# Layer 1's weight transfers on GpSimd's queue, one weight chunk made per block, and most convolution taps in the block-end step

## The chip, the cores and the metric

The kernel runs on one core of a Trainium2 chip. The metric is the time of one execution on the device in microseconds, as the median of several runs. Engines are named as in the profile: PE is TensorE, DVE is VectorE, ACT is ScalarE, POOL is GpSimd, and SP is the engine whose queue issues nearly all DMA transfers. SPq is that queue.

## The reference

A causal convolution with seven softmaxed taps per head runs over 8192 tokens of 192 features. Two layers follow, each with 2048 hidden units: the first with SiLU, the second with ELU.

```python
def reference(**kwargs):
    attn_out = _attn_ref(**attn_kwargs)        # softmax(weight) taps over 7 tokens, per head
    x = attn_out.reshape(B * S, D)             # 8192 x 192
    x = _moe_ref(x=x, **moe_kwargs)            # h = x @ w_in; (h * sigmoid(h)) @ w_out
    return _moe2_ref(x=x, **moe2_kwargs)       # h = x @ w_in; (h if h > 0 else exp(h) - 1) @ w_out
...
```

The kernel splits each float32 operand into a high and a low part and adds up three products (high by high, and the two mixed ones).

## The kernel before

**Tiling.** The tokens are cut into 16 blocks of 512 (`TB`), the hidden units into 8 chunks of 256 (`NQ`). A unit is (layer, block, chunk), and there are 256 of them. A *step* is what the main loop emits for one unit: the products h of this unit with the first weights (`in_products`, 18 of L547), the activation and the split of its result (`act_steps`), and the products of an earlier unit with the second weights. The units run in this order: blocks 0 and 1 of layer 0 together, chunk by chunk (steps 0 to 15); then blocks 2 to 15 of layer 0, 8 steps each (steps 16 to 127); then layer 1's 16 blocks (steps 128 to 255). In a block, q counts the chunks.

**Two forms.** Up to block 2 the low part of the hidden values is kept in float32 form (`g_lo`, L576, products at L720 and L628). From block 3 on it is scaled to a half-precision number (`lo`, L584) and multiplied later: `high_products` (L647) run three steps after the unit's h, and once a block, in the step with q = 2 of the next block, the low parts of all eight chunks follow (`low_products`, L659 for c and L671 for ab). This is the *block-end step*. In it, ScalarE and VectorE also add up the two row halves of the sums (`end_steps`, L771 and L762; `emit_end_c`, L796 and L798) and store them (L376, L380). The hidden values h have two buffers in PSUM. A buffer is free when VectorE's `lo` has read it, so the products of step s wait for `lo` of step s - 2.

**Scales.** The scale of a block's hidden values comes from a bound. `measure` (L428) takes the maxima of a block on each partition, `share` (L418) stores them, `fetch` (L422) brings all of them to every partition, and `set_scale` (L451 to L459) computes from them. The weights' maxima go the same way (`set_weight_scale`, `finish_weight_scale`). Layer 0's second weights are scaled afterwards, one chunk per step, in `rescale` (L245 to L251) and `rescale_end` (L257).

**Side work.** A table `fill` holds, for each step, small pieces of work that are emitted there, ahead of the step's activation, in the order in which `at` was called. These are, for each block b with first step s of layer 0: its input's load at s - 14; the 14 taps of its convolution (`conv_steps`: 7 of 512 columns, 7 of 256, L500 and L502), `measure` and the split into high and low parts (`split_conv`, L156 and L159), spread evenly over the seven steps from s - 10; `fetch` at s - 3; `set_scale` at s - 1. The crossings of x_hl (L315) copy one half of the partitions to the other, by SP.

**Layer 1's weights** arrive as float64 (I64 words) and are decoded on the chip. From step 40 on, each chunk is loaded and its maximum found (`load_w`, `measure_raw`, every third step). From step 72 on, every fifth step, a chunk is loaded again, decoded and split (`made_steps`, nine pieces in five steps), in a single pair of tiles (wi, wo). It is stored to DRAM (L203) and, when layer 0 is done with its own chunk, brought back in its place (`bring`, L221). The copy into wi (L364) of one chunk has to wait until the store of the chunk before has read the tile.

**Order.** The order is written out by hand, and each engine runs its instructions in program order, SP's queue too. For blocks 0 and 1, the two row halves use one bank in turn, and SP does a `nop` as a marker between them (L729), which TensorE waits for. `pair_end` (L743 to L749) ends these two blocks; its tile `other` has one buffer.

Of the kernel before, what the change touches and what calls it, by code (L numbers as in the profile page):

```python
# [9 lines left out]
F32 = mybir.dt.float32  # L10
# [35 lines left out]
def kernel(  # L46
# [48 lines left out]
    def w_loads(layer, q):  # L95
        w = weights[layer]

        def rows_of(i):
            if i == 0:
                raw_t[layer, q] = raw.tile([P, W_IN + W_OUT], I64, tag="raw", name="raw")  # L100
            nc.sync.dma_start(
                out=raw_t[layer, q][ROWS[i], 0 : 2 * P].rearrange("p (k m) -> p k m", k=2),
                in_=w[:, q, ts(i, P)].rearrange("(k p) m -> p k m", k=2),
            )

        def rest(cols):
            nc.sync.dma_start(out=raw_t[layer, q][:, cols], in_=w[:, q, cols])
# [73 lines left out]
    def made_steps(q):  # L181
# [15 lines left out]
        def send():  # L197
            if q == 0:
                wt[1, 0] = [wi, wo]
                return  # L200
            for n, t in (("wi", wi), ("wo", wo)):
                kept[n, q] = tc.dram_tile([P, 2, t.shape[2]], F32, name=f"kept_{n}")
                nc.sync.dma_start(out=kept[n, q], in_=t.bitcast(F32))  # L203

# [12 lines left out]
    def bring(q, k):  # L217
        name, n = (("wi", W_IN), ("wo", W_OUT))[k]
        t = wts.tile([P, 2, n], F32R, tag=f"{name}{q - 1}", name=name)
        wt.setdefault((1, q), [None, None])[k] = t  # L220
        nc.sync.dma_start(out=t.bitcast(F32), in_=kept[name, q])  # L221

# [32 lines left out]

# [158 lines left out]

    def share(key, t):

        shared[key] = tc.dram_tile([1, 2 * P], F32, name="shared")
        nc.sync.dma_start(out=shared[key].rearrange("a (p n) -> (a p) n", n=2), in_=t)  # L418

    def fetch(key):  # L420
        t = fixed.tile([P, 2 * P], F32, tag="all", name="all")
        nc.sync.dma_start(out=t, in_=shared[key].to_broadcast([P, 2 * P]))  # L422
        shared[key] = t
# [37 lines left out]
    def set_weight_scale(layer, of):  # L461
# [3 lines left out]
        if layer == 1:  # L465
# [3 lines left out]
            )  # L469
        share(layer, m)  # L470

# [228 lines left out]
    def pair_products(b, q):  # L700
# [37 lines left out]
        return [[lambda r=r, n=n: product(r, n) for n in range(len(order))] for r in range(2)]  # L738

    def pair_end(b):  # L740

        at, away = ROWS[:: 1 - 2 * b]
        c, ab = (acc_t.pop((0, b, name)) for name in ("c", "ab"))  # L743
        other = out_p.tile([P, TB], F32, tag="other", name="other")[at, :]
        copy(other, c[away, :])
# [68 lines left out]

    def at(step, f):
        fill.setdefault(max(step, 0), []).append(f)

# [23 lines left out]
    for b in range(2, NB):  # L841
        s = where[0, b, 0]
        if b > 2:
            at(s - 14, lambda b=b: pending.extend(x_loads(b)) if b < 5 else load_x(b))
        steps = [f for fs in zip(*(conv_steps(b, g) for g in range(2))) for f in fs]
        if b >= NEW:
            steps += [lambda b=b: measure(0, b, conv_t[b, 0], conv_t[b, 1])]
            at(s - 3, lambda b=b: fetch((0, b)))
            at(s - 1, lambda b=b: set_scale(0, b))
        steps += [lambda b=b, g=g: split_conv(b, g) for g in range(2)]  # L850
        spread(steps, *((s - 10, 7) if b > 2 else (s - 10, 8)))
# [17 lines left out]
    look += 3 * NQ  # L869
    at(look, lambda: set_weight_scale(1, found))  # L870
    at(look + 2, lambda: fetch(1))
    at(look + 4, lambda: finish_weight_scale(1))
# [12 lines left out]
    with tc.manual_schedule():  # L885
# [179 lines left out]
        for s in range(4, TWO + 3):  # L1065
# [24 lines left out]
        act = act_steps(units[TWO + 3])  # L1090
        run(fill.get(TWO + 3, ()))
        run(act)
# [3 lines left out]
        for s in range(TWO + 4, n_units):  # L1096
# [7 lines left out]
            act = act_steps(u)  # L1104
            if s == turn:
                run(fill.get(s, ()))
                run(act)
                continue
            done = units[s - (LATE if turn < s < n_units - 3 else LAG)]
            new = scaled(*done[:2])  # L1110
            if done[2] < NQ - 1:
                run(fill.get(s, ()))
                run(act)
                products(high_products(done) if new else out_products(done))
                continue
            if new:
                run(act)
                products(high_products(done))
# [6 lines left out]
            if not new:  # L1125
                run(act[1:])
            if u[0] == 0:
                end_ab()
                run(fill.get(s, ()))
            else:  # L1130
                run(fill.get(s, ()))
                end_ab()
            emit_end_c(*done[:2], both)

        products(high_products(units[-2]))
# [54 lines left out]
```

## Time and profile before

| | us |
|---|---|
| median of 3 runs | 1121.72 (1120.26 to 1122.46) |
| the profiled execution | 1120.85 |
| its span, first to last instruction | 1118.8 |
| PE busy | 1084.3 (97%) |
| DVE busy | 823.4 (74%) |
| ACT busy | 809.8 (72%) |
| POOL busy | 34.4 (3%) |
| mean granted PE clock | 0.991 of 2.4 GHz |

A busy PE is one with a matmul in flight. PE is busy in nearly every slice, so the 3% in which it is not, and the slower stretches behind them, are where time can be found without less work. Of DMA transfers, all go over one hardware queue, 81.17 MB, which takes 28.8% of the time of the 16 DMA engines. POOL works in the first 75 us only and issues no transfers.

### The profile page before, as it was taken

The numbers are of one execution on the slowest core, as the hardware profiler recorded it, in microseconds if no ns is written. First come the engines' busy times: TensorE is split into PE (matmuls) and PEld (weight loads), VectorE is DVE, ScalarE is ACT, GpSimd is POOL, SyncE is SP. The second block draws the span as 40 slices with busy tenths as digits, with TensorE's granted clock in tenths as the row PEclk, the third lists the DMA queues.
The fourth block names the chain that finished last, engine by engine and source line by source line (L and its number), as shares of the span: only waits on it lengthen the run. The fifth ranks groups of instructions, "written<-read, shape, count | busy, mean of one in ns | idle before, by whom it ended". The sixth has DMA issues, their size and how long they took to land.

```text
span 1118.8 us, 25134 instructions
## 1 busy us (share of the span) xinstructions
PE 1084.3 (97%) x10755; PEld 838.9 (75%) x10755; DVE 823.4 (74%) x1141; ACT 809.8 (72%) x899; POOL 34.4 (3%) x43
## 2 busy tenths in 40 slices
PE   9998899999998988999999999999999999999998
PEld 6887888676775666767877777787777778777776
DVE  8897867676685676776547777777777777777776
ACT  7765656555565575766668888888888898888885
POOL 4420000000000000000000000000000000000000
PEclk9999999999999898999999999999999999999999
DMA  5413113632435137331363212122221212222100
GB/s 156 129 44 76 35 34 91 130 89 80 117 95 149 56 90 172 70 105 39 81 202 97 58 36 54 27 57 58 58 57 35 47 36 57 57 59 57 35 13 23
DMA packets 54048, 82.77 MB, mean 74 GB/s; under 512 B 10800, under 2 KB 27312, under 8 KB 53936
## 3 DMA queue, kind: packets, MB, share of 16 engines
q1 hardware_dynamic: 53936, 81.17, 28.8%
q8 instruction: 84, 1.38, 0.6%
q14 instruction: 28, 0.23, 0.1%
HBM read 43.23 MB, written 18.12 MB: 55 GB/s over the span
## 4 chain that ended last, share of the span: by engine, by line
PE 76%; DVE 10%; DMA 6%; ACT 3%; issue 2%; SPq 2%; DVEq 0%; ACTq 0%
PE h L547 37%; PE ab L647 14%; PE ab L671 9%; PE c L647 7%; PE c L659 5%; DVE lo L584 3%; DVE conv L502 2%; DMA all<-shared 2%; DMA kept_wi<-wi 2%; PE ab L720 2%; PE c L720 1%; DMA x_hl<-x_hl 1%; DMA shared<-sum 1%; PE ab L628 1%; ACT g_hi L581 1%
## 5 line engine op out<-in xcount | busy, mean ns | idle before, releaser
L547 PE MATMUL h<-x_hl,wi 64*128 64x512 f32 x4464 | 583.2, 393 | 26.5 <-DVE lo L584 25.4
L547 PEld LDWEIGHTS h<-x_hl,wi 64*128 64x128 f32 x4464 | 440.7, 186 | 129.4 <-DVE lo L584 34.9
L593 DVE SCALAR_TENSOR_TENSOR g<-g,h 128x1024 f32<-128x1024 f32 x128 | 156.3, 1221 | 129.8 <-ACT g L592 129.8
L647 PE MATMUL ab<-g_hi,wo 64*128 64x512 f32 x1856 | 249.5, 388 | 0.0
L647 PEld LDWEIGHTS ab<-g_hi,wo 64*128 64x128 f32 x1856 | 176.0, 185 | 36.1
L584 DVE SCALAR_TENSOR_TENSOR lo<-h,forth,g_hi 128x1024 f16<-128x1024 f32 x104 | 133.2, 1281 | 76.7 <-ACT g_hi L581 76.3
L589 ACT ACTIVATE h<-h 128x1024 f32<-128x1024 f32 x104 | 104.8, 1007 | 100.3 <-PE h L547 99.1
L584 DVE SCALAR_TENSOR_TENSOR lo<-g,forth,g_hi 128x1024 f16<-128x1024 f32 x128 | 163.6, 1278 | 0.1
L591 ACT ACTIVATE g<-h 128x1024 f32<-128x1024 f32 x128 | 131.7, 1029 | 42.9 <-PE h L547 42.9
L647 PE MATMUL c<-g_hi,wo 64*128 64x512 f32 x928 | 144.2, 389 | 0.0
L581 ACT ACTIVATE g_hi<-g,forth 128x1024 fp32r<-128x1024 f32 x126 | 143.1, 1136 | 0.0
L592 ACT ACTIVATE g<-g 128x1024 f32<-128x1024 f32 x128 | 135.7, 1060 | 4.0
L581 ACT ACTIVATE g_hi<-h,forth 128x1024 fp32r<-128x1024 f32 x104 | 116.1, 1116 | 3.4
L502 DVE SCALAR_TENSOR_TENSOR conv<-x_raw,tap_w,conv 128x512 f32<-128x512 f32 (+1 forms) x174 | 103.1, 632 | 0.2
L647 PEld LDWEIGHTS c<-g_hi,wo 64*128 64x128 f32 x928 | 88.1, 186 | 18.5 <-issue 0.4
L671 PE MATMUL ab<-lo,w 64*64 64x512 f16 x1792 | 101.5, 376 | 0.0
L671 PEld LDWEIGHTS <-w 64*64 64x64 f16 x1920 | 56.0, 107 | 44.3
L659 PE MATMUL c<-lo,w 64*64 64x512 f16 x928 | 55.9, 379 | 0.0
L659 PEld LDWEIGHTS <-w 64*64 64x64 f16 x928 | 24.6, 107 | 27.6 <-issue 10.6
L574 ACT ACTIVATE g_hi<-h 128x1024 fp32r<-128x1024 f32 x22 | 22.5, 1024 | 27.9 <-PE h L547 27.9
L720 PE MATMUL ab<-g_hi,wo 64*128 64x512 f32 x128 | 35.4, 395 | 0.0
L771 ACT ACTIVATE o<-ab,back 128x512 f32<-128x512 f32 x16 | 11.0, 688 | 32.1 <-PE ab L671 27.0
(121 smaller groups left out, 764.6 us busy)
## 6 DMA issues: line engine op xcount, KB each, us to landing
x_hl<-x_hl SPq DMA_DIRECT2D x60, 256.0 KB, 3.8
raw<-in_w_dram SPq DMA_DIRECT2D x21, 512.0 KB, 5.5
raw<-in_w_dram SPq DMA_DIRECT2D x51, 128.0 KB, 4.0
x_raw<-in_xT_dram SPq DMA_DIRECT2D x16, 259.0 KB, 3.9
kept_ab<-mid_ab SPq DMA_DIRECT2D x16, 256.0 KB, 2.1
mid_ab<-kept_ab SPq DMA_DIRECT2D x16, 256.0 KB, 5.2
mid_c<-kept_c SPq DMA_DIRECT2D x32, 128.0 KB, 4.8
all<-shared SPq DMA_DIRECT2D x31, 128.0 KB, 4.3
```

The source lines that it names most:

```text
L502: nc.vector.scalar_tensor_tensor(out=y, in0=x, scalar=w, in1=y, op0=ALU.mult, op1=ALU.add)
L547: nc.tensor.matmul(out=h[:, r, :], lhsT=w[ROWS[r], w_lo, ts(of, P)], rhs=x_part(layer, b, 3 * x_lo + part)[ROWS[r], :], start=n == 0, stop ...
L581: nc.scalar.activation(out=hi, in_=g, func=ACTF.Copy, scale=s)
L584: nc.vector.scalar_tensor_tensor(out=lo, in0=g, scalar=s, in1=hi.bitcast(F32), op0=ALU.mult, op1=ALU.subtract)
L589: return [lambda: nc.scalar.activation(out=g, in_=h, func=ACTF.Silu), high, low]
L591: lambda: nc.scalar.activation(out=g, in_=h, func=ACTF.Relu, scale=-1.0),
L592: lambda: nc.scalar.activation(out=g, in_=g, func=ACTF.Exp, scale=-1.0),
L593: lambda: nc.vector.scalar_tensor_tensor(out=g, in0=g, scalar=-1.0, in1=h, op0=ALU.add, op1=ALU.max),
L647: nc.tensor.matmul(out=acc_t[layer, b, f"{name}{r}"], lhsT=wo[ROWS[r], i, ts(k, P)], rhs=hi[ROWS[r], i, :], start=q == 0 and n in (0, 2), ...
L659: nc.tensor.matmul(out=acc_t[layer, b, f"c{r}"][ROWS[i], :], lhsT=w16_t[layer, q][ROWS[r], i, P:D], rhs=g_t[u][1][ROWS[r], i, :], start=Fa ...
L671: nc.tensor.matmul(out=bank[ROWS[j], :], lhsT=w16_t[layer, q][ROWS[r], i, ts(j, HP)], rhs=g_t[u][1][ROWS[r], i, tokens], start=first and i ...
L720: ins = nc.tensor.matmul(out=acc_t[0, b, name][0 : cols.stop - cols.start, :], lhsT=wo[ROWS[r], i, cols], rhs=g_t[0, b, q][part][ROWS[r], ...
```

## The change

Layer 1's loads of weights, its stores of made chunks and the transfers that bring them back are issued by GpSimd. So are `share` and `fetch` of the two weight scales. The fill table gets three parts per step. In a block-end step, part 0 runs ahead of the activation (blocks of layer 0 in the old form: after it), part 1 between the end of c and the end of ab, and part 2 at the end of the step; in other steps the three run one after the other where the table ran before.

From block 5 on, two taps of the convolution run at q = 0 and q = 1 of the block before, and the other 12 in its block-end step: three in part 0, five in part 1, four in part 2. `measure` follows at q = 3, the split at q = 4. Block 4 keeps its even spread of taps over seven steps, with `measure`, split and `fetch` one step later. Layer 1's chunks are measured at eight chosen steps from 37 to 49, and one chunk is made per block from block 8 on (steps 61 to 122).

In `rescale`, the scaling of the low part goes to ScalarE and the addition to GpSimd; before, VectorE did both in one operation for each of two ranges. In `pair_end` both blocks use one tile.

```diff
     def w_loads(layer, q):
         w = weights[layer]
+        queue = nc.gpsimd if layer else nc.sync
...
-            nc.sync.dma_start(
+            queue.dma_start(
...
-                nc.sync.dma_start(out=kept[n, q], in_=t.bitcast(F32))
+                nc.gpsimd.dma_start(out=kept[n, q], in_=t.bitcast(F32))
...
-        nc.sync.dma_start(out=t.bitcast(F32), in_=kept[name, q])
+        nc.gpsimd.dma_start(out=t.bitcast(F32), in_=kept[name, q])
...
+        nc.scalar.activation(out=wo[:, :, D : 2 * D], in_=wo[:, :, D : 2 * D].bitcast(F32), func=ACTF.Copy, scale=up[0])
         for src, to in LOWS:
-            nc.vector.scalar_tensor_tensor(
-                out=wo[:, :, to], in0=wo[:, :, to].bitcast(F32), scalar=up[0], in1=more[:, :, src],
-                op0=ALU.mult, op1=ALU.add,
-            )
+            nc.gpsimd.tensor_add(out=wo[:, :, to], in0=wo[:, :, to].bitcast(F32), in1=more[:, :, src])
...
-        share(layer, m)
+        share(layer, m, nc.gpsimd)
...
+        if b == 0:
+            others.append(out_p.tile([P, TB], F32, tag="other", name="other"))
+        other = others[0][at, :]
...
-    def at(step, f):
-        fill.setdefault(max(step, 0), []).append(f)
+    def at(step, f, part=0):
+        fill.setdefault((max(step, 0), part), []).append(f)
...
+        if b <= 3:
+            spread(steps + found_it * (b == NEW) + splits, s - 10, 7 if b > 2 else 8)
+        elif b == 4:
+            spread(steps, s - 10, 7)
+            at(s - 4, found_it[0])
+        else:
+            for k, f in enumerate(steps):
+                step = s - 8 if k < 1 else s - 7 if k < 2 else s - 6
+                at(step, f, 0 if k < 5 else 1 if k < 10 else 2)
+            at(s - 5, found_it[0])
+        if b >= 4:
+            for f in splits:
+                at(s - 4 + (b == 4), f)
         if b >= NEW:
-            at(s - 3, lambda b=b: fetch((0, b)))
+            at(s - 3 + (b == 4), lambda b=b: fetch((0, b)))
             at(s - 1, lambda b=b: set_scale(0, b))
...
-        at(where[1, b, 0] - 6, lambda b=b: split_mid(b))
+        at(where[1, b, 0] - 6, lambda b=b: split_mid(b), 1)
...
-    at(TWO + 1, lambda: fetch(0))
+    at(TWO + 1, lambda: fetch(0, nc.gpsimd))
...
-    look = where[0, 5, 0]
-    for q in range(NQ):
-        at(look + 3 * q, lambda q=q: load_w(1, q))
-        at(look + 3 * q + 3, lambda q=q: measure_raw(q))
+    looks = [where[0, b, q] for b, q in ((4, 5), (4, 6), (5, 0), (5, 1), (5, 5), (5, 6), (6, 0), (6, 1))]
+    for q, s in enumerate(looks):
+        at(s - 4, lambda q=q: load_w(1, q), 2)
+        at(s, lambda q=q: measure_raw(q))
...
-        s = look + 8 + 5 * k
-        at(s - 7, lambda q=q: load_w(1, q))
-        at(s, lambda q=q: made.update({q: made_steps(q)}))
-        for i in range(9):
-            at(s + i // 2, lambda q=q, i=i: made[q][i]())
+        s = where[0, 8 + k, 0]
+        at(s - 10, lambda q=q: load_w(1, q), 2)
+        at(s - 4, lambda q=q: made.update({q: made_steps(q)}))
+        for i, step in enumerate((-3, -2, -1, 0, -1, -1, 1, 1, 2)):
+            at(s + step, lambda q=q, i=i: made[q][i](), 2 * (step == 2))
...
             if new:
+                run_fill(s, 0)
                 run(act)
                 products(high_products(done))
                 low_products(*done[:2])
...
             end_c()
             if not new:
                 run(act[1:])
-            if u[0] == 0:
-                end_ab()
-                run(fill.get(s, ()))
-            else:
-                run(fill.get(s, ()))
-                end_ab()
+                run_fill(s, 0)
+            run_fill(s, 1)
+            end_ab()
             emit_end_c(*done[:2], both)
+            run_fill(s, 2)
```

## Rows read from the trace of the kernel before

**Rows 1.** The chain that ended last: start us, us, what.
```profile
165.94 3.45 PE ab L671 x64
...
338.05 3.51 PE ab L671 x64
...
527.29 3.45 PE ab L671 x64
...
560.01 3.51 PE ab L671 x64
...
593.55 3.45 PE ab L671 x64
...
1084.45 3.45 PE ab L671 x64
```

**Rows 2.** Waits: who waited for whom, us in total, times, longest us.
```profile
PE h L547 <- DVE lo L584: 25.4, 18, 5.6
...
ACT wi L364 <- DMA kept_wi<-wi: 18.6, 4, 7.6
...
DVE total L451 <- DMA all<-shared: 7.3, 4, 2.1
```

**Rows 3.** Timeline, 340 to 366: start, us, engine, line, instruction, [idle before <- releaser].
```profile
364.70 1.65 PE L547 MATMUL h<-x_hl,wi 64*128 64x512 f32 x6 [5.63 <-DVE lo L584]
```

**Rows 4.** Stretch 364 to 369: PE, PEld, DVE, ACT, POOL busy, granted clock, DMA.
```profile
364.00:369.00 5.00, 4.30 (x20) 3.47 (x22) 4.83 (x12) 2.46 (x4) 0.00 (x0) 0.50 0.10 42
```

**Rows 5.** Timeline of PE and of SP's queue, steps 16 to 18.
```profile
77.96 0.39 PE L547 MATMUL h<-x_hl,wi 64*128 64x512 f32 x1
...
82.26 0.39 PE L547 MATMUL h<-x_hl,wi 64*128 64x512 f32 x1
...
86.21 0.34 SPq L418 DMA_DIRECT2D shared<-own  x1
...
86.66 0.49 PE L720 MATMUL c<-g_hi,wo 64*128 64x512 f32 x1 [2.18 <-SPq L729]
...
90.43 0.60 PE L547 MATMUL h<-x_hl,wi 64*128 64x512 f32 x1
```

**Rows 6.** Timeline of ACT and PE where `pair_end` runs.
```profile
96.58 0.59 ACT L364 ACTIVATE other<-c 64x512 f32<-64x512 f32 x1 [3.77 <-DMA kept_c<-other]
...
97.94 0.73 PE L628 MATMUL c<-g_hi,wo 64*128 64x512 f32 x3 [0.76 <-DVE other L746]
```

**Rows 7.** Timeline of DVE and PE at steps 26 to 28.
```profile
136.38 0.75 DVE L251 SCALAR_TENSOR_TENSOR wo<-wo,up,more 128x128 fp32r<-128x128 f32 x2
...
138.38 3.91 PE L547 MATMUL h<-x_hl,wi 64*128 64x512 f32 x18 [3.98 <-DVE lo L584]
```

**Rows 8.** Timeline of DVE and POOL, 24 to 56.
```profile
42.70 2.11 DVE L502 SCALAR_TENSOR_TENSOR conv<-x_raw,tap_w,conv 128x512 f32<-128x512 f32 x2
...
43.61 1.79 POOL L174 TENSOR_TENSOR wo<-val,wo 128x128 fp32r<-128x128 f32 x2
...
48.69 1.14 DVE L502 SCALAR_TENSOR_TENSOR conv<-x_raw,tap_w,conv 128x512 f32<-128x512 f32 x2
```

**Rows 9.** Timeline around the block-end step of block 14 of layer 0.
```profile
526.31 1.28 DVE L584 SCALAR_TENSOR_TENSOR lo<-h,forth,g_hi 128x1024 f16<-128x1024 f32 x1 [2.11 <-ACT g_hi L581]
...
531.50 0.75 DVE L762 SCALAR_TENSOR_TENSOR mid_ab<-ab,back,mid_ab 128x512 f32<-128x512 f32 x1 [2.70 <-ACT mid_ab L771]
532.17 1.80 DVE L502 SCALAR_TENSOR_TENSOR conv<-x_raw,tap_w,conv 128x512 f32<-128x512 f32 x3
...
534.20 2.20 PE L547 MATMUL h<-x_hl,wi 64*128 64x512 f32 x18
...
535.81 1.27 DVE L584 SCALAR_TENSOR_TENSOR lo<-h,forth,g_hi 128x1024 f16<-128x1024 f32 x1
...
537.60 2.20 PE L547 MATMUL h<-x_hl,wi 64*128 64x512 f32 x18
```

**Rows 10.** Groups by line: xcount | busy us, mean ns of one | idle before.
```profile
L148 DVE SCALAR_TENSOR_TENSOR val<-mag,val 128x768 int32<-128x768 int32 x12 | 11.5, 958 | 1.3
```

More of the change, by code (lines that the diff above doesn't have):

```diff
@@ L106, in rest @@
         def rest(cols):
-            nc.sync.dma_start(out=raw_t[layer, q][:, cols], in_=w[:, q, cols])
+            queue.dma_start(out=raw_t[layer, q][:, cols], in_=w[:, q, cols])
         parts = (slice(2 * P, W_IN), OUT) if layer == 0 and q < RAW else (slice(2 * P, W_IN + W_OUT),)
@@ L413, with share, fetch @@
     shared = {}
-    def share(key, t):
+    def share(key, t, queue=nc.sync):
         shared[key] = tc.dram_tile([1, 2 * P], F32, name="shared")
-        nc.sync.dma_start(out=shared[key].rearrange("a (p n) -> (a p) n", n=2), in_=t)
-    def fetch(key):
+        queue.dma_start(out=shared[key].rearrange("a (p n) -> (a p) n", n=2), in_=t)
+    def fetch(key, queue=nc.sync):
         t = fixed.tile([P, 2 * P], F32, tag="all", name="all")
-        nc.sync.dma_start(out=t, in_=shared[key].to_broadcast([P, 2 * P]))
+        queue.dma_start(out=t, in_=shared[key].to_broadcast([P, 2 * P]))
         shared[key] = t
@@ L738, in pair_products @@
         return [[lambda r=r, n=n: product(r, n) for n in range(len(order))] for r in range(2)]
+    others = []
     def pair_end(b):
@@ L743, in pair_end @@
         c, ab = (acc_t.pop((0, b, name)) for name in ("c", "ab"))
-        other = out_p.tile([P, TB], F32, tag="other", name="other")[at, :]
+        if b == 0:
+            others.append(out_p.tile([P, TB], F32, tag="other", name="other"))
+        other = others[0][at, :]
         copy(other, c[away, :])
@@ L813, with run_fill @@
     fill = {}
-    def at(step, f):
-        fill.setdefault(max(step, 0), []).append(f)
+    def at(step, f, part=0):
+        fill.setdefault((max(step, 0), part), []).append(f)
+    def run_fill(s, *parts):
+        for part in parts or range(3):
+            run(fill.get((s, part), ()))
     def spread(steps, first, n):
@@ L845 @@
         steps = [f for fs in zip(*(conv_steps(b, g) for g in range(2))) for f in fs]
+        found_it = [lambda b=b: measure(0, b, conv_t[b, 0], conv_t[b, 1])]
+        splits = [lambda b=b, g=g: split_conv(b, g) for g in range(2)]
+        if b <= 3:
[11 more added lines that the diff above has]
+                at(s - 4 + (b == 4), f)
         if b >= NEW:
-            steps += [lambda b=b: measure(0, b, conv_t[b, 0], conv_t[b, 1])]
-            at(s - 3, lambda b=b: fetch((0, b)))
+            at(s - 3 + (b == 4), lambda b=b: fetch((0, b)))
             at(s - 1, lambda b=b: set_scale(0, b))
-        steps += [lambda b=b, g=g: split_conv(b, g) for g in range(2)]
-        spread(steps, *((s - 10, 7) if b > 2 else (s - 10, 8)))
     for b in range(NB):
         at(where[1, b, 0] - 9, lambda b=b: load_mid(b))
-        at(where[1, b, 0] - 6, lambda b=b: split_mid(b))
+        at(where[1, b, 0] - 6, lambda b=b: split_mid(b), 1)
         at(where[1, b, 0] - 4, lambda b=b: fetch((1, b)))
@@ L864 @@
         at(TWO + LAG + 2 + q, lambda q=q: rescale_end(q))
-    look = where[0, 5, 0]
-    for q in range(NQ):
-        at(look + 3 * q, lambda q=q: load_w(1, q))
-        at(look + 3 * q + 3, lambda q=q: measure_raw(q))
[L869 to L872, printed above, removed]
+    looks = [where[0, b, q] for b, q in ((4, 5), (4, 6), (5, 0), (5, 1), (5, 5), (5, 6), (6, 0), (6, 1))]
+    for q, s in enumerate(looks):
+        at(s - 4, lambda q=q: load_w(1, q), 2)
+        at(s, lambda q=q: measure_raw(q))
+    look = looks[-1]
+    at(look + 1, lambda: set_weight_scale(1, found))
+    at(look + 3, lambda: fetch(1, nc.gpsimd))
+    at(look + 5, lambda: finish_weight_scale(1))
     made = {}
     for k, q in enumerate([*range(1, NQ), 0]):
-        s = look + 8 + 5 * k
-        at(s - 7, lambda q=q: load_w(1, q))
-        at(s, lambda q=q: made.update({q: made_steps(q)}))
-        for i in range(9):
-            at(s + i // 2, lambda q=q, i=i: made[q][i]())
+        s = where[0, 8 + k, 0]
[3 more added lines that the diff above has]
+            at(s + step, lambda q=q, i=i: made[q][i](), 2 * (step == 2))
     base = where[0, NB - 1, 0]
@@ L1082 @@
                 pending.extend(w_loads(0, s + 1))
-            run(fill.get(s, ()))
+            run_fill(s)
             run(act[-1:] if s < 6 else act)
@@ L1090 @@
         act = act_steps(units[TWO + 3])
-        run(fill.get(TWO + 3, ()))
+        run_fill(TWO + 3)
         run(act)
@@ L1104 @@
             act = act_steps(u)
-            if s == turn:
-                run(fill.get(s, ()))
-                run(act)
-                continue
             done = units[s - (LATE if turn < s < n_units - 3 else LAG)]
             new = scaled(*done[:2])
-            if done[2] < NQ - 1:
-                run(fill.get(s, ()))
+            if s == turn or done[2] < NQ - 1:
+                run_fill(s)
                 run(act)
-                products(high_products(done) if new else out_products(done))
+                if s != turn:
+                    products(high_products(done) if new else out_products(done))
                 continue
             if new:
+                run_fill(s, 0)
                 run(act)
@@ L1126 @@
                 run(act[1:])
-            if u[0] == 0:
-                end_ab()
-                run(fill.get(s, ()))
-            else:
-                run(fill.get(s, ()))
-                end_ab()
+                run_fill(s, 0)
+            run_fill(s, 1)
+            end_ab()
             emit_end_c(*done[:2], both)
+            run_fill(s, 2)
         products(high_products(units[-2]))
```

## The prediction

> **What bounds the kernel now.** First I read the chain that ended last. It is TensorE nearly throughout, so I looked for the stretches in which TensorE is not fed. In that chain the last products of a block (ab L671, 64 of them) return once per block, and their distances show the pace. [rows 1] From 593.55 to 1084.45 there are 15 blocks of layer 1: 490.90 / 15 = 32.73 us each. One block of layer 0, from 527.29 to 560.01, takes the same 32.72 us, with all its convolution work. So 32.73 is what TensorE needs, and layer 0 can reach it. The 12 blocks of layer 0 from 165.94 to 593.55 took 427.61 us, that is 427.61 - 12 x 32.73 = **34.9 us more** than TensorE needs: 8.5 in the first five (338.05 - 165.94 - 163.65) and 26.4 in the other seven, where layer 1's weights are made.
>
> What feeds TensorE late is read from the waits. [rows 2] Its products h wait 25.4 us in all for VectorE's lo (L584): h has two buffers, and VectorE frees one when it has read it. VectorE works in program order, so lo is late whenever something ahead of it waits: ScalarE waits 18.6 us, 7.6 at the longest, to copy into the weight tile wi (L364), which a store to DRAM (L203) must have read before; VectorE waits 7.3 us for fetched maxima (L451). In the timeline the longest of these waits leaves TensorE without work for 5.63 us before the products at 364.70. [rows 3] After it the granted clock is 0.50, the 1.2 GHz level, for 5 us [rows 4], in which half a clock loses 2.5 us more. One event costs some 8 us.
>
> **The change part by part.** The sum is made against the profiled execution, 1120.85 us (its span is 1118.8, with 2.05 around it); the median of the three runs is 1121.72, 0.87 above.
>
> *Layer 0's weight maxima on GpSimd's queue.* Step 17 takes 90.43 - 82.26 = 8.17 us, the step ahead of it 82.26 - 77.96 = 4.30. [rows 5] TensorE stood 2.18 us for a marker on SP's queue (L729), and its products come slower after that. The marker stood behind the store of the maxima, which goes out only at 86.21, when VectorE has made them. On another queue the store holds no marker up: **-3.9**.
>
> *One tile for both halves in pair_end.* ScalarE waits 3.77 us until the first half's store has read the shared tile, and TensorE stands 0.76 us for the sum behind it. [rows 6] Without the wait the bank is free in time: **-0.8**. Against that stands that the fetch through GpSimd now gates the rescaling. TensorE is 3.9 us earlier there and VectorE waits in order; no row has a transfer from GpSimd, so between 0 and 2 us, and I take **+1.0**.
>
> *Rescaling.* VectorE gives up two operations, 0.75 us together [rows 7], for each of eight chunks; ScalarE gets one more and GpSimd two adds, 1.79 us a pair as its subtractions go. [rows 8] At 4.30 us a step nothing there stops TensorE; what counts is the turn to the half-precision low parts, where TensorE stands 3.98 us for lo. [rows 7] Two chunks lie ahead of it there, so at most 1.5 is given back. But GpSimd's adds slow VectorE: two taps take 1.14 us alone and 2.11 beside those subtractions. [rows 8] I take **-1.0** of a possible 0 to -4.0.
>
> *Taps, measuring and splitting at fixed steps.* In the block-end step TensorE has 5.5 us of low products more (32.73 less eight steps of 3.40, which is 537.60 - 534.20), and VectorE two holes: 2.11 us before lo, 2.70 us before mid_ab. [rows 9] Three taps of two sizes take 1.80 and a pair 1.14. [rows 8, 9] Part 0 (three taps) fits the first hole. Part 1 (five taps) takes two pairs and a short one, 2.5 to 2.8 with their overlap: it just fills the second. Part 2 (four taps) stands where today three taps and a fourth stand behind mid_ab. So the next lo should start where it does now, at 535.81, and end 0.5 us before the products at 537.60 need its buffer. Nothing is won or lost in a quiet block, but the other steps are nearly empty of taps.
>
> *Layer 1's chunks.* A chunk was made every five steps wherever it fell; now one per block, with at most two of its VectorE operations in a step. The longest of them is 0.96 us [rows 10], so 1.92 beside lo's 1.28 [rows 9] in a step of 3.40. The copy that waited now comes five steps behind the last write to the tiles that the store reads, one of them the block end: 5 x 3.40 + 5.5 = 22.5 us. Loads are asked for four steps before they are measured and seven before they are decoded, at least 13.6 us.
>
> *The 80 transfers that leave SP* (48 loads, 14 stores, 14 brings, 4 of maxima) no longer stand ahead of the crossings of x_hl and the fetches of each block. New waits: on GpSimd's queue a load waits for its raw tile, and what is queued behind it is loads and stores with the slack just named; nobody else waits for GpSimd there. I therefore give back all 34.9 of the blocks: **-34.9**.
>
> *New costs.* For block 4 the measuring moves one step closer to its use (three steps, 10.2 us), while the first three loads leave GpSimd at once and share the DMA engines with its crossings: 0 to 3, taken as **+1.5**. At each of eight block ends a pair of stores and a load come from GpSimd just when the twelve taps run. No row has that; from below it is 0, from above every pair is hit like the one beside the subtractions: 6 x 0.97 less the 0.5 of slack, 5.3 us a block or 42 in all. The nearest row is that of a GpSimd operation that reads two tiles, which a transfer's issue is not, so I stay close to the lower end: 0.3 a block, **+2.4**.
>
> There the Trainium skill bears on it, too. "SBUF — State Buffer", section "Who interferes with whom", says that VectorE with two SBUF inputs contends with GpSimd only where GpSimd reads, and infers that making descriptors needs the write side. By that rule this term would be 0 and the time 2.4 us lower; the slowed taps beside the subtractions agree with its first half, and no row here shows the second.
>
> **Sum:** -3.9 - 0.8 + 1.0 - 1.0 - 34.9 + 1.5 + 2.4 = -35.7, so 1085.2 in the profiled execution's terms and, with the 0.87, **1086** by the median.
>
> **Rivals.**
> 1. *GpSimd's queue slows VectorE at the block end.* For: the doubled pair of taps [rows 8], a slack of only 0.5 us, and TensorE's lower clock after a long stall. Against: those were arithmetic. With half of the pairs hit: 3 x 0.97 - 0.5 = 2.4 a block, 19 over eight blocks, 1086 + 19 - 2.4 = **1103**; a quarter and three quarters of them give 1092 and 1115.
> 2. *The crossings stay late.* The 8.5 us of the first five blocks are put down to landings, of the fetched maxima [rows 2] and of the transfers around them, and the bytes that are moved stay the same. If they all stay: 1086 + 8.5 = **1094**. "DMA: Bandwidth & Descriptors" of the Trainium skill, section "Issuing engines are not separate DMA queues", says that all queues run on the same 16 engines and a second one saves only issuing time; by that rule alone this rival would hold, and the time would be 1094. Here TensorE's stand on a marker [rows 5] shows a wait in SP's order, which a second queue does remove, so I give it little.
> 3. *Slower: stores from GpSimd starve.* If GpSimd needs so long for a store that it has not read wi at the next copy, every chunk repeats the event described above, 8 us each [rows 3, 4], seven times: 1086 + 56 = **1142**. It decides from 22.5 us per store; the longest wait on such a store is 7.6 us now, with stores every five steps. [rows 2]
> 4. *The holes are not there.* If a stall merely moves to the crowded block-end step, where twelve taps now crowd the buffers of h, all of the 34.9 may come back: 1086 + 35 = **1121**. Against it stands the count of the holes above.
>
> **Chances and range.** Forecast, 1078 to 1092: 0.60. Contention, 1092 to 1115: 0.21. Late crossings, about 1094: 0.07. No change: 0.04. Slower: 0.08. About 0.2%, 2.2 us, is what a measurement here can tell from none. So faster 0.88, same 0.04, slower 0.08. Low end: every term at its best, -3.9 - 0.8 - 4.0 - 34.9 = -43.6, 1078 by the median, and 1 less for the spread of the runs (1120.26 to 1122.46). High end: it takes in the late crossings and the half-hit block ends, 1103, and some of what lies beyond them, to leave out no more than 0.2: 1107. **Range 1077 to 1107.**
>
> **What would show it.** In the chain of waits of the changed kernel the L671 groups of layer 0 should stand 32.7 to 33.1 us apart from the second such block on; the waits should have no copy on ScalarE behind kept_wi, no marker wait at L729 above 0.5 us and less than 5 us of h behind lo. Taps of over 1 us, or a pair of 2 us, at block ends would show rival 1; h behind x_hl transfers rival 2; a copy behind kept_wi again rival 3. The prediction is wrong if a block of layer 0 with chunks takes over 34.5 us.

## The result and the profile after

| | before | after |
|---|---|---|
| median, us | 1120.99 (1118.04 to 1122.46) | 1081.07 (1080.43 to 1082.08) |
| profiled execution, us | 1120.85 | 1080.66 |
| its span, us | 1118.8 | 1079.0 |
| mean granted PE clock | 0.991 | 0.998 |

The ratio of the times is 0.9648, with a 95% interval of 0.9626 to 0.9670. The forecast was 1086 with a range of 1077 to 1107, so the sign and the range held, and the time came out 5 us below the forecast.

Of the page of the changed kernel, the busy times and the two DMA queues:

```profile
PE 1069.7 (99%) x10755; PEld 842.0 (78%) x10755; DVE 820.0 (76%) x1125; ACT 813.5 (75%) x907; POOL 90.4 (8%) x139
...
q1 hardware_dynamic: 42416, 57.30, 22.0%
q0 software_dynamic: 6240, 23.86, 7.4%
```

PE's busy time fell from 1084.3 to 1069.7 with the same work. By an estimate from the mean clocks, some 8 of these 14.6 us are clock: 0.009 x 1118.8 us were lost to it, and now 0.002 x 1079.0. The larger part of the gain is idle time, now 1% of the span instead of 3%. A new queue, q0, is GpSimd's and carries 23.86 MB.

The chain that ended last (start us, us, what), the last products of a block, as in [rows 1]; the line is now L670:

```profile
159.05 3.45 PE ab L670 x64
191.78 3.51 PE ab L670 x64
225.93 3.45 PE ab L670 x64
...
324.11 3.45 PE ab L670 x64
...
520.47 3.45 PE ab L670 x64
553.50 3.45 PE ab L670 x64
...
1044.40 3.45 PE ab L670 x64
```

Against [rows 1], everything up to the first of these is 165.94 - 159.05 = 6.9 us shorter. The 12 blocks that follow take 553.50 - 159.05 = 394.45 us instead of 427.61, **33.2 us less**. They stand 1.7 us above 12 x 32.73, 1.4 of it in the block from 191.78 to 225.93, which takes 34.15. The 15 blocks of layer 1 take 490.90 us in both kernels. So the gain is 40.1 us, and all of it lies in layer 0.

The waits (who waited for whom: us in total, times, longest us):

```profile
POOL kept_wi L204 <- DVE wi L366: 212.7, 7, 50.0
POOL kept_wo L204 <- ACT h L588: 19.2, 7, 2.8
DVE total L450 <- DMA all<-shared: 5.7, 3, 3.1
PE h L546 <- DVE lo L583: 2.7, 1, 2.7
PE h L546 <- DMA x_hl<-x_hl: 1.4, 2, 1.1
```

Products h waited 25.4 us for `lo` [rows 2], and now wait once, 2.7 us. No copy on ScalarE waits for a store any more. GpSimd's queue waits 212.7 us ahead of its stores, and that costs nothing: only loads and stores with slack stand behind.

### The profile page after: what moved, and what is told of

It reads as the page before. It is cut to its first block, busy times and chain, and to the rows that moved or that the text cites. A ratio compares the mean times of both kernels' runs of the same rounds, so it can differ in the third digit from the quotient of the medians.

```text
span 1079.0 us, 25189 instructions
## 1 busy us (share of the span) xinstructions
PE 1069.7 (99%) x10755; PEld 842.0 (78%) x10755; DVE 820.0 (76%) x1125; ACT 813.5 (75%) x907; POOL 90.4 (8%) x139
## 3 DMA queue, kind: packets, MB, share of 16 engines
q0 software_dynamic: 6240, 23.86, 7.4%
## 4 chain that ended last, share of the span: by engine, by line
PE 96%; DVE 1%; ACT 1%; DMA 1%; SPq 0%; issue 0%; POOL 0%; DVEq 0%; POOLq 0%
PE h L546 47%; PE ab L646 19%; PE c L646 10%; PE ab L670 9%; PE c L658 5%; PE ab L719 2%; PE c L719 1%; DMA x_hl<-x_hl 1%; PE ab L627 1%; PE c L627 1%; SPq L314 0%; PE warm L909 0%; PE conv_ps L940 0%; PE last L670 0%; DVE conv L501 0%
## 5 line engine op out<-in xcount | busy, mean ns | idle before, releaser
L546 PE MATMUL h<-x_hl,wi 64*128 64x512 f32 x4464 | 574.5, 389 | 4.1 <-DVE lo L583 2.7
L670 PE MATMUL ab<-lo,w 64*64 64x512 f16 x1792 | 101.5, 376 | 0.0
L670 PEld LDWEIGHTS <-w 64*64 64x64 f16 x1920 | 55.9, 107 | 44.4
```

What stands on the lines that cost most here:

```text
L546: nc.tensor.matmul(out=h[:, r, :], lhsT=w[ROWS[r], w_lo, ts(of, P)], rhs=x_part(layer, b, 3 * x_lo + part)[ROWS[r], :], start=n == 0, stop ...
L670: nc.tensor.matmul(out=bank[ROWS[j], :], lhsT=w16_t[layer, q][ROWS[r], i, ts(j, HP)], rhs=g_t[u][1][ROWS[r], i, tokens], start=first and i ...
```

## The experiments

For a finer account than the blocks, the *excess* below is the time of steps 28 to 130, each from its first product h to the next one's in the timeline, above 8.80 us for a block-end step, 3.53 for the one behind it and 3.40 for the others (together 32.73 a block). It was 36.6 us before and is 3.5 after.

### What carries the blocks

Three things were changed there at once: the queue, the spacing of the chunks, and the packed taps. Four kernels take them apart.

**The queue put back on SP** in the changed kernel:

```diff
-        queue = nc.gpsimd if layer else nc.sync
+        queue = nc.sync
...
-                nc.gpsimd.dma_start(out=kept[n, q], in_=t.bitcast(F32))
+                nc.sync.dma_start(out=kept[n, q], in_=t.bitcast(F32))
...
-        nc.gpsimd.dma_start(out=t.bitcast(F32), in_=kept[name, q])
+        nc.sync.dma_start(out=t.bitcast(F32), in_=kept[name, q])
```

> The changed kernel with the 76 transfers of layer 1's weights back on SP's queue; the fill table stays as changed. Theory A (the place of the pieces in the fill table carries most of the gain, since the copy now comes 22.5 us behind the store it waits for): 1081 to 1088, no wait of ScalarE for kept_wi, only a few microseconds of late crossings in blocks 5 to 8. Rival (the queue carries it: crossings and fetches stand behind loads and stores in SP's order): 1095 or more, with products h waiting for x_hl transfers or for lo behind fetched maxima in many blocks.

Measured: 1078.42 us, a ratio of 0.9626 (0.9600 to 0.9652) to the kernel before, with 1.0 us of excess. The gain doesn't need GpSimd's queue for these 76 transfers once the work is placed as it is now (the four of the weight scales stayed on it).

**The queue alone**, in the kernel before (the same three edits, the other way round):

> The kernel before with those 76 transfers on GpSimd's queue and nothing else. Theory A: the stores go out sooner and land in under 3 us as in the changed kernel, so the 18.6 us of ScalarE's wait for kept_wi shrink to under 3 and the blocks lose perhaps half of their 34.9 us: 1098 to 1110; what stays are steps in which a chunk's pieces meet the taps. Rival (the queue carries all of the blocks' gain): 1086 to 1092. Rival (the queue carries none): 1118 or more.

Measured: 1112.42 us, 0.9926 (0.9898 to 0.9954), between theory A and the rival that gives the queue nothing. The copies no longer wait for the store and the excess falls to 23.0, but 11.3 us of waits for fetched maxima (7.3 before) and 5.9 for crossings are there, and step 16 takes 11.59 us instead of 4.30. Half of that comes back at once: step 17, with its marker, takes 4.31 instead of 8.17. The timeline of this kernel shows why: PE's products of step 16, and GpSimd's and SP's issues ahead of them.

```profile
70.47 4.90 SPq L316 DMA_DIRECT2D x_hl<-x_hl  x4
70.90 1.39 POOL L102 DMA_DIRECT2D raw<-in_w_dram  x2
...
83.01 0.79 PE L548 MATMUL h<-x_hl,wi 64*128 64x512 f32 x1 [4.32 <-DMA x_hl<-x_hl]
```

The loads of layer 1, written out for step 40 and later, leave at 70.90, the moment when GpSimd's arithmetic ends, because nothing else stands in its queue. They meet the crossings of block 2. By stretches (busy times of PE, PEld, DVE, ACT, POOL, then granted clock, DMA share and GB/s) the DMA engines are full from 74 to 84; three of these stretches:

```profile
76.00:78.00 2.00, 2.00 (x20) 2.00 (x19) 2.00 (x4) 0.00 (x0) 0.58 (x1) 1.00 0.99 297
78.00:80.00 2.00, 0.69 (x7) 0.22 (x3) 2.00 (x5) 1.94 (x2) 0.00 (x0) 1.00 1.03 251
80.00:82.00 2.00, 0.00 (x0) 0.00 (x0) 2.00 (x5) 0.00 (x0) 0.00 (x0) 0.95 1.05 259
```

In the kernel before, the DMA share is 0.00 from 78 to 84. On SP's queue the order holds these loads back.

What the queue gives is an earlier store. In the kernel before, the store ahead of the copy that waits 7.64 us leaves 18.3 us after VectorE's last write to the tile, and lands 8.4 us later. In this kernel the store of the same chunk leaves 0.3 us after that write and lands in 2.6. First the kernel before, then this one:

```profile
333.42 0.55 DVE L367 TENSOR_TENSOR wi<-val,wi 128x384 fp32r<-128x384 f32 x1
...
352.24 0.63 SPq L203 DMA_DIRECT2D kept_wi<-wi  x1
...
360.74 0.52 ACT L364 ACTIVATE wi<-val 128x384 fp32r<-128x384 f32 x1 [7.64 <-DMA kept_wi<-wi]
```

```profile
335.04 0.55 DVE L368 TENSOR_TENSOR wi<-val,wi 128x384 fp32r<-128x384 f32 x1
...
335.88 0.56 POOL L204 DMA_DIRECT2D kept_wi<-wi  x1 [34.98 <-DVE wi L368]
```

**A chunk every five steps**, with GpSimd's queue and the packed taps:

```diff
-        s = where[0, 8 + k, 0]
-        at(s - 10, lambda q=q: load_w(1, q), 2)
-        at(s - 4, lambda q=q: made.update({q: made_steps(q)}))
-        for i, step in enumerate((-3, -2, -1, 0, -1, -1, 1, 1, 2)):
-            at(s + step, lambda q=q, i=i: made[q][i](), 2 * (step == 2))
+        s = look + 8 + 5 * k
+        at(s - 7, lambda q=q: load_w(1, q), 2)
+        at(s, lambda q=q: made.update({q: made_steps(q)}))
+        for i in range(9):
+            at(s + i // 2, lambda q=q, i=i: made[q][i]())
```

> The changed kernel with a chunk made every five steps, wherever it falls, as before. Theory A: the store through GpSimd lands fast enough, so ScalarE's wait for kept_wi is under 3 us in all; but a chunk's VectorE pieces fall into block-end steps whose holes the taps have filled: 3 to 12 us more, 1084 to 1093. Rival (five steps are too few for any store): ScalarE waits over 10 us for kept_wi and the time is 1095 or more. Rival (the spacing did nothing): 1081.

Measured: 1089.95 us, 0.9723 (0.9698 to 0.9748), excess 12.7. So spacing is worth some 9 us with this queue. No copy waits for a store here either. At the first steps of three blocks (48, 64 and 80) 4.8 us are lost behind fetches and crossings (DVE total for all: 13.8 us in all; h for x_hl: 4.0); at steps 68, 84 and 93 it is 3.3 us, behind the pieces of a chunk. None of the late steps is a block end, where the expectation had put them.

**Five steps and SP's queue**, both edits:

> The changed kernel with a chunk every five steps and with the transfers of layer 1's weights back on SP's queue, so both ways of getting a store out in time are undone. Theory B (either way alone is enough for the wait of ScalarE on kept_wi; that is why undoing the queue alone cost nothing): the wait returns with over 10 us in all and the time is 1098 to 1112. Theory A alone (the spacing beside the taps matters, the store wait does not): about that of the run with five steps on GpSimd's queue, 1090, less the 2 us that SP's queue gave: 1086 to 1091.

Measured: 1091.88 us, 0.9739 (0.9720 to 0.9759), excess 15.0, just above the range of theory A and below that of B. The store comes back as a cause, but for two copies only, 8.6 us in all. The longer wait, from this kernel's timeline:

```profile
339.75 0.67 SPq L204 DMA_DIRECT2D kept_wi<-wi  x1
...
346.95 0.52 ACT L363 ACTIVATE wi<-val 128x384 fp32r<-128x384 f32 x1 [6.50 <-DMA kept_wi<-wi]
...
350.90 4.21 PE L546 MATMUL h<-x_hl,wi 64*128 64x512 f32 x18 [4.49 <-DVE lo L583]
```

Steps 79 and 80 are 7.3 us over their floor, about the 8 us that the prediction read from the event before 364.70 [rows 3, 4]. Against that, the waits for fetched maxima fall from 13.8 to 3.3 us. In this spacing the two queues come to within 2 us of each other: one makes a store late, the other fetches.

**The taps spread evenly** over seven steps again, with measuring and splitting behind them, in the changed kernel:

```diff
-            for k, f in enumerate(steps):
-                step = s - 8 if k < 1 else s - 7 if k < 2 else s - 6
-                at(step, f, 0 if k < 5 else 1 if k < 10 else 2)
-            at(s - 5, found_it[0])
+            for k, f in enumerate(steps + found_it + splits):
+                step = s - 10 + k * 7 // 17
+                at(step, f, 2 * (step == s - 6))
-        if b >= 4:
+        if b == 4:
```

> The changed kernel with the taps, the measuring and the splitting of blocks 5 to 15 spread over seven steps as before, those of the block-end step at its end. Theory A: a chunk's pieces meet 1.1 us of taps per step, 1.6 + 1.1 + 1.3 us in a step of 3.4, so VectorE's lo comes late in the eight blocks with chunks: 3 to 10 us more, 1084 to 1091, none in blocks 14 and 15's neighbours without chunks. Rival (packing the taps did nothing, the other parts suffice): 1081 to 1082.

Measured: 1084.63 us, 0.9678 (0.9648 to 0.9707), excess 7.2. By the excess, packing the taps is worth 3 to 4 us: 2.3 at steps 32, 48 and 56, where layer 1 is loaded and measured (3.7 over the floor there, less the 1.4 of the changed kernel), the rest some 0.15 in a later block. The first part is not shown to be the packing's, for it varies from run to run: a second profile of the changed kernel (last experiment) has 0.75 at step 32 and 0.73 at step 48, and the kernel with the maxima on SP's queue (below), with packed taps too, has 2.7 at these two. The intervals of the two ratios, 0.9648 to 0.9707 and 0.9626 to 0.9670, overlap as well.

Side by side, the excess in us:

| chunks | taps | SP's queue | GpSimd's queue |
|---|---|---|---|
| every 5 steps | spread | 36.6 (before) | 23.0 |
| every 5 steps | packed | 15.0 | 12.7 |
| one a block | spread | not run | 7.2 |
| one a block | packed | 1.0 | 3.5 (after) |

(With the packed taps go the new places of measuring, splitting and of layer 1's first loads, and the parts of the change outside these steps; these were not taken apart further. The largest step in the table, 36.6 to 15.0, is theirs together.) Step 28 has 1.6 to 1.8 in each of these but the 1.0, where it has 0.1 for a reason of its own (last section). Read by rows: the queue is worth 13.6 in the crowded schedule, 2.4 in between, and -0.9 in the calm one (0.8 against 1.7 without step 28). Read downwards, again without step 28: on SP's queue the schedule alone takes 34.9 to 0.8. The parts don't add up: they remove in part the same late steps.

### The three small parts

**Layer 0's maxima on SP's queue:**

```diff
-        share(layer, m, nc.gpsimd)
+        share(layer, m, nc.gpsimd if layer else nc.sync)
...
-    at(TWO + 1, lambda: fetch(0, nc.gpsimd))
+    at(TWO + 1, lambda: fetch(0))
```

> The changed kernel with the store and the fetch of layer 0's weight maxima back on SP's queue. If the markers of step 17 stood behind that store: TensorE stands 2 us for L728 again, step 17 takes 8.2 us, the time is 3.9 us more, 1085. If the marker was late for another reason: 1081.

Measured: 1084.15 us, 0.9664. The timeline shows [rows 5] again, almost to the digit; step 17 goes from 82.00 to 90.50, 8.50 us:

```profile
82.00 0.39 PE L546 MATMUL h<-x_hl,wi 64*128 64x512 f32 x1
...
86.07 0.34 SPq L417 DMA_DIRECT2D shared<-own  x1
...
86.51 0.56 PE L719 MATMUL c<-g_hi,wo 64*128 64x512 f32 x1 [2.19 <-SPq L728]
...
90.50 0.39 PE L546 MATMUL h<-x_hl,wi 64*128 64x512 f32 x1
```

In the changed kernel the same two rows are 82.08 and 86.38, so the step takes 4.30 us; the store waits on GpSimd's queue, where nobody stands behind it:

```profile
82.08 0.39 PE L546 MATMUL h<-x_hl,wi 64*128 64x512 f32 x1
...
86.34 0.72 POOL L417 DMA_DIRECT2D shared<-own  x1 [15.65 <-DVE own L463]
86.38 0.39 PE L546 MATMUL h<-x_hl,wi 64*128 64x512 f32 x1
```

**pair_end with a tile per half:**

```diff
-        if b == 0:
-            others.append(out_p.tile([P, TB], F32, tag="other", name="other"))
-        other = others[0][at, :]
+        other = out_p.tile([P, TB], F32, tag="other", name="other")[at, :]
```

> The changed kernel with a tile of its own for each half in pair_end, in one buffer. Step 19 goes from 6.57 back to 7.3 to 8.0 us: 1082 to 1082.5. If the wait of ScalarE for the first store is covered now that step 17 is shorter: no step changes.

Measured: 1086.11 us, 0.9683 (0.9664 to 0.9703). That is 5 us more, where the prediction had 0.8. The timeline:

```profile
94.28 0.59 ACT L363 ACTIVATE other<-c 64x512 f32<-64x512 f32 x1 [5.26 <-DMA kept_c<-other]
...
95.66 0.83 PE L627 MATMUL c<-g_hi,wo 64*128 64x512 f32 x3 [2.67 <-DVE other L747]
```

ScalarE waits 5.26 us where it waited 3.77, and TensorE stands 2.67 where it stood 0.76 [rows 6]. The store that ScalarE waits for takes 3.90 us to land, 90.28 to 94.18, where it took 2.40, 94.07 to 96.47. With the marker's stall gone it leaves 3.8 us earlier and meets the fetch of the maxima, which leaves 1.0 us later than before. These two transfers, in this kernel and in the kernel before:

```profile
90.05 0.56 POOL L421 DMA_DIRECT2D all<-shared  x1 [2.93 <-DMA shared<-own]
90.28 0.49 SPq L379 DMA_DIRECT2D kept_c<-other  x1
```

```profile
89.06 0.33 SPq L422 DMA_DIRECT2D all<-shared  x1
...
94.07 0.49 SPq L380 DMA_DIRECT2D kept_c<-other  x1
```

In the three kernels here in which the fetch leaves 4.7 us or more ahead of this store, the store lands in 2.40 to 2.42 us; in the eleven in which both leave within 0.4 us, it takes 3.9 to 5.1, but for one with 2.44. That the two share the DMA engines fits this, and no run separates it. Behind the idle time the clock in 95 to 100 is 0.66, where it was 1.00 in 97 to 102 of the kernel before, and the step takes 11.27 us instead of 6.57.

**Rescaling on VectorE, as before:**

```diff
-        nc.scalar.activation(out=wo[:, :, D : 2 * D], in_=wo[:, :, D : 2 * D].bitcast(F32), func=ACTF.Copy, scale=up[0])
         for src, to in LOWS:
-            nc.gpsimd.tensor_add(out=wo[:, :, to], in0=wo[:, :, to].bitcast(F32), in1=more[:, :, src])
+            nc.vector.scalar_tensor_tensor(
+                out=wo[:, :, to], in0=wo[:, :, to].bitcast(F32), scalar=up[0], in1=more[:, :, src],
+                op0=ALU.mult, op1=ALU.add,
+            )
```

> The changed kernel with the rescaling as before: VectorE does scaling and addition, GpSimd and ScalarE nothing of it. TensorE's idle time at the turn (step 28) was 3.98 before and is 2.73. If the two operations that left VectorE there made the difference: 4.0 again and 1 to 2 us more. If GpSimd's adds slow the taps as much as they relieve VectorE: 2.7 or less, no change.

Measured: 1081.56 us, 0.9647: no difference that can be told. Steps 26 and 27 take 9.10 us together instead of 8.54, so the part is worth 0.6 in the profile. TensorE's idle time at the turn is 2.96 us, between the 4.0 and the 2.7 of the two expectations.

### Does GpSimd's queue slow VectorE?

Two kernels put far more on GpSimd beside the taps of 11 block ends: ten additions of 160 columns each, or eight more stores of 32 KB each. Both are additions to the changed kernel that nothing reads.

```diff
+    def beside(u):
+        for _ in range(10):
+            nc.gpsimd.tensor_add(out=spare[:, 0, :], in0=spare[:, 1, :], in1=g_t[u][1][:, 0, 0:160])
...
+                if u[0] == 0 and s < where[0, 15, 0]:
+                    beside(units[s - 1])
```

```diff
+    def beside(u):
+        for k in range(8):
+            spare = tc.dram_tile([P, 128], F16, name="spare")
+            nc.gpsimd.dma_start(out=spare, in_=g_t[u][1][:, k // 4, ts(k % 4, P)])
...
+                if u[0] == 0 and s < where[0, 15, 0]:
+                    beside(units[s - 1])
```

> The changed kernel with ten GpSimd additions of 160 columns, two inputs in SBUF, beside the taps of each of the eleven block-end steps 34 to 114 (they write a spare tile; the output is the same). If GpSimd's reads hold up VectorE's taps: taps of 512 columns of 1.0 us and more at the block ends instead of 0.74, lo late, 1 to 4 us per block, 1092 to 1125. If the doubled taps seen early in the kernel had another cause: 1081.

> The changed kernel with eight more transfers from GpSimd, stores of 32 KB to DRAM, beside the taps of each of the eleven block-end steps 34 to 114. Rival 1 of the prediction (issuing from GpSimd slows the taps): taps longer than 0.76 us at block ends, 1 to 4 us per block, 1092 to 1125. If making descriptors doesn't touch the taps: taps of 0.74 and 0.48, 1081 to 1084, where the extra is only what the bytes do to crossings.

Measured, from two runs each: 1082.47 us (0.9665) with the additions, 1079.69 us (0.9640) with the stores. The same block end in both, DVE's three taps of part 0 and five of part 1 with POOL's work beside them; first with additions, then with stores (the taps are L506 here):

```profile
320.81 2.27 DVE L506 SCALAR_TENSOR_TENSOR conv<-x_raw,tap_w,conv 128x512 f32<-128x512 f32 x3
321.04 6.80 POOL L263 TENSOR_TENSOR spare<-spare,lo 128x160 f32<-128x160 f32 x10 [23.27 <-DVE lo L588]
...
325.41 3.37 DVE L506 SCALAR_TENSOR_TENSOR conv<-x_raw,tap_w,conv 128x256 f32<-128x256 f32 x5
```

```profile
320.18 1.80 DVE L506 SCALAR_TENSOR_TENSOR conv<-x_raw,tap_w,conv 128x512 f32<-128x512 f32 x3
320.56 4.25 POOL L263 DMA_DIRECT2D spare<-lo  x8 [25.64 <-DVE lo L588]
...
324.79 2.59 DVE L506 SCALAR_TENSOR_TENSOR conv<-x_raw,tap_w,conv 128x256 f32<-128x256 f32 x5
324.80 0.54 POOL L204 DMA_DIRECT2D kept_wi<-wi  x1
```

Three taps take 1.80 us beside the issues, which is [rows 9], and 2.27 beside additions; five take 2.59 and 3.37. Over all block ends a tap of 512 columns takes 0.747 us beside an issue (median of 44), 0.739 alone, and 0.973 beside an addition (44 taps). Issuing transfers from GpSimd slows these taps by no more than 0.008 us in the median. That is what the Trainium skill ("SBUF — State Buffer", "Who interferes with whom") infers for descriptors, and its first half, that VectorE with two inputs contends with a GpSimd operation that reads, is in the other kernel's rows.

The additions cost VectorE 0.47 + 0.78 = 1.25 us in two of the parts of a block end, yet each block lost only 0.13 to 0.2: by the difference the block end has about 1 us of slack there, where the prediction had 0.5.

### The change again, and a better version

The changed kernel was timed once more beside the last three:

> The changed kernel as it is, once more, beside the runs of this call. 1081 to 1082 by the earlier runs. Step 28 took 5.1 us in some traces and 3.5 in others behind the same 2.7 us without products; this one shows which of the two it gets again.

Measured: 1081.58 us, 0.9658 (0.9645 to 0.9671). Step 28 takes 5.14 us again.

The last kernel takes the changed one with SP's queue for layer 1 (as above) and moves the last two chunks of the rescaling away from the turn to the half-precision low parts:

```diff
-        at(TWO + LAG + 1 + q, lambda q=q: rescale(q))
-        at(TWO + LAG + 2 + q, lambda q=q: rescale_end(q))
+        s = TWO + LAG + 1 + q + {6: 5, 7: 6}.get(q, 0)
+        at(s, lambda q=q: rescale(q))
+        at(s + 1, lambda q=q: rescale_end(q))
```

> The changed kernel with layer 1's transfers back on SP's queue (as in x1_queue_back, 1078.4) and the rescaling of chunks 6 and 7 moved behind the turn, from steps 25 and 26 to 30 and 32. If VectorE's operations at the turn make lo late: the idle time before step 28 falls from 2.7 to under 1.5 us, the granted clock stays, 1074 to 1077. If something else makes lo late there (the sums of block 2): 2.7 stays, 1078.

Measured: **1076.66 us**, 0.9611 (0.9597 to 0.9624), 5 us below the changed kernel on the same chip. TensorE's idle time at the turn is all but gone. The row of the changed kernel, then of this one:

```profile
131.46 3.44 PE L546 MATMUL h<-x_hl,wi 64*128 64x512 f32 x18 [2.73 <-DVE lo L583]
```

```profile
129.66 2.33 PE L546 MATMUL h<-x_hl,wi 64*128 64x512 f32 x18 [0.69 <-DVE lo L583]
```

## Why the prediction was right, and where not

The sum was -35.7; the chain shows -40.1. By its steps (times of steps that are in no row above are from the starts of h in the same timelines):

- **Maxima, -3.9.** Step 17 went from 8.17 to 4.30, and putting it back costs 3.1 by the medians. Right, and for the reason given.
- **pair_end and the fetch through GpSimd, -0.8 + 1.0.** Step 19, in which [rows 6] lie, went from 7.98 to 6.57, -1.4. The failed step is the size of both terms: VectorE waited only 0.5 us for the maxima fetched through GpSimd, and the one tile is worth 4.7 in this kernel. The prediction took the stall as it stood in the trace (0.76), although its own first term moves the store 3.8 us ahead, beside the fetch. Without the edit, 3.3 of the 3.9 us of the first term would have gone back here (step 19 with 11.27 instead of 7.98).
- **Rescaling, -1.0.** Steps 26 and 27 went from 9.78 to 8.54, -1.2; TensorE's idle time at the turn from 3.98 [rows 7] to 2.73. The run with the old rescaling shows 0.6 of it; where the other 0.6 comes from stays open.
- **Blocks, -34.9 + 1.5 + 2.4 = -31.0.** Measured -33.2. The waits behind the store are gone, and block ends are quiet: 32.73 apart in the chain. But the prediction counted the queue and the schedule as one cause. The runs show that the schedule carries it (34.0 of 34.9 us of excess on SP's own queue, step 28 aside) and that the queue gives nothing on top; alone, in the crowded schedule, it is worth 13.6. Its sentence that 80 transfers no longer stand ahead of the crossings named no gain that needs the queue.
- **Block 4, +1.5.** The size came out, and the place only in part. In the profile of the changed kernel the loads that GpSimd sends early meet the crossings not of block 4 but of block 6, at step 48, 1.4 us over its floor, so that one block takes 34.15 us where the prediction had at most 33.1. In the second profile it is 0.75 at block 4 (step 32) and 0.73 at block 6. From the timeline of the first:

```profile
202.93 4.49 SPq L314 DMA_DIRECT2D x_hl<-x_hl  x3
205.57 1.18 POOL L102 DMA_DIRECT2D raw<-in_w_dram  x2 [17.11 <-DVE found L238]
206.74 0.58 POOL L108 DMA_DIRECT2D raw<-in_w_dram  x1
207.51 0.55 SPq L421 DMA_DIRECT2D all<-shared  x1
...
214.01 1.89 PE L546 MATMUL h<-x_hl,wi 64*128 64x512 f32 x14 [1.10 <-DMA x_hl<-x_hl]
214.28 0.42 DVE L450 TENSOR_REDUCE total<-all 128x1 f32<-128x256 f32 x1 [3.06 <-DMA all<-shared]
```

  With SP's queue step 48 takes 3.44, and steps 32 and 33 are 0.4 us over; the last kernel, on SP's queue too, has 0.7 at step 32. So part of this is not GpSimd's, and that the size agrees is in part luck.
- **GpSimd's issues beside the taps, +2.4.** Measured 0. The doubled pair of taps [rows 8] was no row for it: those were operations that read two tiles.

So 4.4 us were missed: 1.6 at pair_end, 2.2 in the two costs of the blocks, 0.2 in rescaling, 0.4 spread over the start.

Of the rivals, the first (contention) falls with the two kernels of GpSimd's extra work, and its price was too high as well (by its own formula, a quarter of the pairs gives 1091 and not 1092). The second (late crossings) is alive in small: some 1.5 us of it are left in the changed kernel, and with chunks every five steps VectorE waits 11.3 and 13.8 us for fetched maxima with GpSimd's queue, 7.3 and 3.3 with SP's. Of the rule that it leaned on ("DMA: Bandwidth & Descriptors" in the Trainium skill, "Issuing engines are not separate DMA queues": a second queue saves only issuing time), the calm schedule is an example, with 0.8 us of excess on SP's queue against 1.7, step 28 aside; in the crowded one the queue did save more than that, 13.6, since in SP's order the stores left late (up to 18.3 us after the last write to their tile, against 0.3 to 0.6 with GpSimd's queue). The third (starving stores) didn't occur: GpSimd's stores of 384 KB landed 2.6 us after their issue, as the median of seven, and 4.6 at the longest. The fourth (no holes) falls with the excess of 0.0 in nearly all blocks.

## What to carry to other kernels

When a store must have been read before a buffer is written again, give it more distance in the schedule first; with the taps packed that took the excess from 15.0 to 1.0 us on SP's own queue, where the second queue alone took it to 12.7, and with the distance the second queue gave nothing more. When a stall is removed, look at what the work behind it will then run beside: here a store moved ahead to where a fetch was under way, and the stall behind it grew. A queue without work of its own runs ahead of the place where its transfers are written, so look at what its early loads will meet.

## What was not expected of the hardware

The clock behind the idle time at the turn is not settled by that idle time. In stretches of 5 us from the products that follow it (columns as above), the changed kernel, then the one with the maxima on SP's queue:

```profile
131.46:136.46 5.00, 5.00 (x30) 3.98 (x32) 4.26 (x7) 2.59 (x3) 4.87 (x9) 0.66 0.79 222
```

```profile
135.57:140.57 5.00, 5.00 (x44) 4.14 (x46) 4.69 (x8) 3.69 (x5) 5.00 (x9) 1.00 0.75 211
```

The idle time is 2.73 and 2.72 us, the mean granted clock 0.66 of 2.4 GHz and 1.00, and step 28 takes 5.14 and 3.54 us. Among the kernels here with 2.7 to 3.0 us of idle time at this place, both forms occur, with and without transfers at the same time: the DMA share was 0.79 (above) and 0.03 (five steps, SP's queue: clock 0.69) with the lower clock, and 0.75 (above) and 0.02 (the changed kernel with SP's queue) with the full one. So 1.6 us of a difference between two profiles can be this alone; what decides it stays open. It is also part of the gap between the changed kernel and the one with SP's queue: of their 2.8 us in the profiled executions, 1.6 stand at step 28 and 1.4 at step 48, less 0.2 elsewhere.

Additions on GpSimd slow a tap to 0.973 us from 0.739; a store's issue on GpSimd takes 0.54 us of its time, and a tap beside it takes 0.747.
